# One transfer for the first pair's query weights in a cached-attention decode kernel

## The chip, the core and the metric

The kernel runs on one core of one Trainium2 chip. The metric is the device time of one launch in microseconds (us); lower is better. All data are 32-bit floats.

## What is computed

One decode step of a block: layer norm of x, grouped-query attention over a long key and value cache, and beside it a dense layer with the Mish activation; both are added to x.

```python
B, D = 8, 512                       # 8 sequences, one token each
Hq, Hkv, Sk, Dh = 32, 8, 8192, 128  # 4 query heads share one key head
F = 1792

xn = layernorm(x)
q = xn @ wq                                   # wq: 512 x 4096
scores = q . k_cache / sqrt(Dh)               # k_cache: 8 x 8 x 8192 x 128
o = softmax(scores) . v_cache                 # v_cache: the same shape
a = o @ wo                                    # wo: 4096 x 512
h = xn @ w1 + b1
m = (h * tanh(softplus(h))) @ w2
out = x + a + m
```

## The kernel before

**Units and buffers.** The caches hold 512 MB in all, and every byte is read once. The work is cut into 32 units (`UNITS`): unit j takes a pair of key heads (m = j // 8) and one sequence (b = j % 8). A unit's keys are one transfer of 8 MB (128 partitions of 64 KB, `load_unit(kT, ...)`, L131), and its values another. All these transfers are issued by the sync engine (SP), which takes its instructions in order and stops at one whose semaphores are not yet there. One large tile `kv` has room for two and a half such transfers: values at `V_AT`, keys in turn at `K_AT[0]` and `K_AT[1]`, which overlap by half. So the keys of unit j + 1 are issued when half the scores of unit j are done (`scores` is called in two halves), and the values of unit j when the values of unit j - 1 are used up.

**The start is different.** The keys of unit 0 go to the values' place. The first weights of the dense layer, `w1` (3.5 MB, L476), go to the start of `K_AT[0]`'s place, where x and its centred copy `xc` stand until then; its bias `b1` comes through four small GpSimd transfers (L147). The keys of unit 1 go to `K_AT[1]` and the values of unit 0 (in the loop over units) to `V_AT`, when the scores of unit 0 have read the keys there. On SP the order is: first pair's query weights, keys 0, `w1`, keys 1, values 0, keys 2, values 1 and so on.

**The queries.** For each pair of heads, `project(m)` multiplies xn by a 512 x 1024 slice of `wq`, `spread` lays the result out in `qr`, and `key_weights` makes from it the stationary operand `wk` of unit j's scores. For the pairs 1 to 3 the slice comes by `load_q(m)` (L125): one SP transfer of 2 MB into `ws`, 128 partitions of 16 KB, so that partition p holds rows 4p to 4p + 3 of the slice; `project` takes four terms with the transposed activations `xn4`. For pair 0 the slice is split. Rows 0 to 383 come by an SP transfer of 1.5 MB into `ws` (L153, three rows to a partition). Rows 384 to 511 come by four GpSimd transfers of 128 KB (L150), issued in turn with the four for `b1`, into `q0_x`: partitions 64 to 95 of `kv` (`XQ`), four rows to a partition, at the column `XAT`. This is the start of `K_AT[1]`'s place, so the transfer of keys 1 waits until `project(0)` has read `q0_x`. The seven terms of pair 0 take the activations from two further transposed copies, `xn3` and `xnx`, which TensorE and VectorE make beside `xn4` (L208 to L221).

**The rest of a unit.** `softmax`, `values` (for the unit before), `key_weights` (for the next unit), `turn` (transposes the exponentials into the stationary operand `pt8` of the values) and `merge`. In unit 0 the activation of the dense layer, `mish` (L399 to L446), stands between; it uses the place of `w1` as scratch, and keys 2 go there afterwards. After the last unit come the transfers of `wo` and `w2` and two output products.

**Where the work starts.** GpSimd builds an identity and `perm` by memsets behind its eight transfers (L158 to L161); VectorE derives masks from them, and then computes the norm (L188 to L201) together with ScalarE.

Of the kernel before, what the change touches and what calls it, by code (L numbers as in the profile page):

```python
# [8 lines left out]
F32 = mybir.dt.float32  # L9
# [4 lines left out]
P = 128  # L14
B = 8
# [12 lines left out]
BW = 1024  # L28
CC = D // P
# [8 lines left out]
ROW = NB * P * BW // P  # L38
# [10 lines left out]
NJ = PL * HALF  # L49

W2R = 7

D3 = 3
XQ = slice(64, 96)
XAT = ROW + ROW // 2

# [11 lines left out]
def kernel(  # L72
# [12 lines left out]
    nc = tc.nc  # L85
    PSUM = bass.MemoryType.PSUM

    const = ctx.enter_context(tc.tile_pool(name="const", bufs=1))
# [4 lines left out]
    kv = const.tile([P, PLACES], F32, name="kv")  # L93
    ws = const.tile([P, CC * BW], F32, name="ws")
# [4 lines left out]
    M = psum.tile([P, 512], F32, name="m")  # L99
    H = psum.tile([P, 512], F32, name="h")  # L100

    ident = const.tile([P, P], F32, name="ident")
# [7 lines left out]
    gsel = const.tile([B, B, B], F32, name="gsel")  # L110
    xn4 = const.tile([P, CC, B], F32, name="xn4")
    xnT = const.tile([P, CC, B], F32, name="xnT")
    xn3 = const.tile([P, D3, B], F32, name="xn3")
    xnx = const.tile([P, CC, B], F32, name="xnx")
    qr = const.tile([P, DI, H2 * B], F32, name="qr")
    xres = const.tile([P, P], F32, name="xres")
    oT = const.tile([P, NP, H2, B], F32, name="oT")
# [4 lines left out]
    def load_q(m):  # L122

        rows = wq.rearrange("j p f -> (j p f)").rearrange("(m p f) -> m p f", m=NP, p=P)
        nc.sync.dma_start(ws, rows[m])  # L125

    def load_unit(src, j, at):
        m, b = divmod(j, B)
        lo = (b * HKV + 2 * m) * NH * G
        t = kv[:, at : at + ROW]  # L130
        nc.sync.dma_start(  # L131
            t,
            src[lo : lo + NB].rearrange("j p f -> (j p f)").rearrange("(p f) -> p f", p=P),
        )
        return t
# [3 lines left out]
    x_sb, xc, sq = (low[:, i * D : (i + 1) * D] for i in range(3))  # L139
    nc.scalar.dma_start(x_sb, x)  # L140
    b1_sb = kv[:B, W1_AT + 7168 : W1_AT + 7168 + FG // 2]
    q0 = wq[:CC].rearrange("j p f -> (j p) f")
    q0_3 = ws[:, : D3 * BW]
    q0_x = kv[XQ, XAT : XAT + CC * BW]
    for r in range(4):
        n = FG // 8
        nc.gpsimd.dma_start(  # L147
            b1_sb[:, n * r : n * (r + 1)], b1.rearrange("(g c f) -> c g f", g=B, c=4)[r]
        )
        nc.gpsimd.dma_start(  # L150
            q0_x[r::4], q0[D3 * P :].rearrange("(e r i) f -> r e (i f)", r=4, i=CC)[r]
        )
    nc.sync.dma_start(q0_3, q0[: D3 * P].rearrange("(p i) f -> p (i f)", i=D3))  # L153
    k_t = {0: load_unit(kT, 0, V_AT)}
    w1_t = kv[:, W1_AT : W1_AT + 7168].rearrange("p (j f) -> p j f", j=2 * CC)

# [47 lines left out]
    for c in range(CC):  # L204
        nc.tensor.transpose(
            M[:, 32 + c * B : 32 + (c + 1) * B], xc[:, c * P : (c + 1) * P], ident[:B, :B]
        )
    for c in range(D3):  # L208
        nc.tensor.transpose(
            M[:, 64 + c * B : 64 + (c + 1) * B], xc[:, c : D3 * P : D3], ident[:B, :B]  # L210
        )
    for c in range(CC):
        nc.tensor.matmul(
            M[XQ, 96 + c * B : 96 + (c + 1) * B],
            xc[:, D3 * P + c :: CC],
            ident[:B, :B],
            start=True,
            stop=True,
        )
    nc.vector.tensor_copy(xn3.rearrange("p c b -> p (c b)"), M[:, 64 : 64 + D3 * B])  # L220
    nc.vector.tensor_copy(xnx[XQ].rearrange("p c b -> p (c b)"), M[XQ, 96:128])  # L221
    nc.vector.tensor_copy(xn4.rearrange("p c b -> p (c b)"), M[:, 0:32])
    nc.vector.tensor_copy(xnT.rearrange("p c b -> p (c b)"), M[:, 32:64])
    for g in range(G):
# [4 lines left out]
            start=True,  # L229
            stop=True,  # L230
# [14 lines left out]
    def project(m):  # L245

        w = ws.rearrange("p (c f) -> p c f", c=CC)
        terms = [(c, xn4[:, c, :], w[:, c]) for c in range(CC)]
        if m == 0:
            wx = q0_x.rearrange("p (c f) -> p c f", c=CC)  # L250
            terms = [(c, xn3[:, c, :], w[:, c]) for c in range(D3)]
            terms += [((c + D3) % CC, xnx[XQ, c, :], wx[:, c]) for c in range(CC)]
        for d in range(2):
            for n, (c, xt, wt) in enumerate(terms):
                nc.tensor.matmul(  # L255
                    H[Q * c : Q * c + B, :],
                    xt,
                    wt[:, d * 512 : (d + 1) * 512],
                    start=(n < CC),
                    stop=(n >= len(terms) - CC),  # L260
                )
            qp = work.tile([P, 512], F32, name="e")
            nc.scalar.copy(qp, H)
            for h in range(REP):
                at = 192 + (d * REP + h) * B
                nc.tensor.matmul(  # L266
                    M[:, at : at + B],
                    qp[:, h * DH : (h + 1) * DH],
                    bsel[:, :B],
                    start=True,  # L270
                    stop=True,
                )
        qT = work.tile([P, H2 * B], F32, name="qT", bufs=1)
        nc.vector.tensor_scalar_mul(qT, M[:, 192 : 192 + H2 * B], DH**-0.5)
        return qT
# [199 lines left out]

    nc.sync.dma_start(w1_t, w1.rearrange("j p f -> p j f"))  # L476
    qT = project(0)
    k_t[1] = load_unit(kT, 1, K_AT[1])
    spread(qT)
# [3 lines left out]
    for j in range(UNITS):  # L483
        b = j % B
# [23 lines left out]
        if more and b == MAKE_Q:  # L508
            qT = project(j // B + 1)
# [29 lines left out]
    for g in range(G):  # L539
# [4 lines left out]
            start=False,  # L544
            stop=False,
# [44 lines left out]
```

## Time and profile before

| | |
|---|---|
| median of three runs | 1333.28 us (1331.31 to 1333.68) |
| the profiled execution | span of 1330.5 us from first to last instruction; the runs shown are 0.8 to 3.2 us above it, their median 2.8 us |
| moved from and to memory | 561.79 MB, a mean of 422 GB/s over the span |
| TensorE busy with matmuls | 984.8 us, 74% |
| VectorE busy | 516.0 us, 39% |
| ScalarE, GpSimd busy | 40.2 us, 6.4 us |

In the profile PE is TensorE (PEld its weight loads), DVE VectorE, ACT ScalarE, POOL GpSimd, SP the sync engine; SPq stands for an instruction that SP issues, and L131 is line 131 of the kernel. A row of the timeline has its start and its length in us, then engine, line, operation, what is written and read, and how many instructions were merged in the row; in brackets follows how long the engine had been idle and what released it. A row of the windows has the stretch, its length, the busy time of each engine (with the number of instructions), the granted TensorE clock, the busy share of the 16 DMA engines, and what they moved in GB/s; bytes are put down where a packet ends, so short stretches scatter. A row of transfers has the count, the size of each and the median time from issue to landing.

### The profile page before, as it was taken

To read this page: it belongs to the slowest core of one execution; us is meant where nothing else is said; L and a number is where in the kernel's file an instruction comes from. 1 tells how busy PE (TensorE), PEld (TensorE's weight loads), DVE (VectorE), ACT (ScalarE), POOL (GpSimd) and SP (SyncE) were. 2 spreads that over 40 slices of the span, in tenths; PEclk is the share of its full clock that TensorE was granted. 3 is DMA by queue.
4 is the path that set the end of the run, shared out by engine and by line. 5 is a ranking of instruction groups with operands and counts; after the bars stand their busy time and mean duration, and the time that the engine had idled before them with its cause. 6 is when DMAs were issued, how large, how long until landed. Compare 5 with 4: busy or idle time off the path is not lost.

```text
span 1330.5 us, 11234 instructions
## 1 busy us (share of the span) xinstructions
PE 984.8 (74%) x5071; PEld 338.3 (25%) x5071; DVE 516.0 (39%) x730; ACT 40.2 (3%) x88; POOL 6.4 (0%) x17
## 2 busy tenths in 40 slices
PE   1888776877867976776887777687786787677766
PEld 0422222222322222222322222222232222222222
DVE  2065444134443234444244444413444332444431
ACT  1000000000000000000000000000000000000000
POOL 1000000000000000000000000000000000000000
PEclk9999789988889888879988888998897998888898
DMA  9889999999999999999999999999999999999997
GB/s 341 338 346 432 420 438 436 436 428 436 428 436 434 434 432 428 427 439 438 426 432 432 438 430 434 426 438 434 430 430 434 432 434 436 428 428 434 430 415 321
DMA packets 13839, 561.79 MB, mean 422 GB/s; under 512 B 1464, under 2 KB 1592, under 8 KB 4800
## 3 DMA queue, kind: packets, MB, share of 16 engines
q1 hardware_dynamic: 13520, 560.53, 98.2%
q8 instruction: 39, 0.64, 0.2%
q0 software_dynamic: 256, 0.53, 0.1%
q10 hardware_dynamic: 16, 0.02, 0.0%
q14 instruction: 8, 0.07, 0.0%
HBM read 561.01 MB, written 0.07 MB: 422 GB/s over the span
## 4 chain that ended last, share of the span: by engine, by line
DMA 73%; PE 22%; DVE 2%; SPq 2%; issue 0%; POOL 0%; ACT 0%; DVEq 0%; POOLq 0%
DMA kv<-in_v 70%; PE o L378 19%; DMA kv<-in_wq 2%; DMA kv<-in_w 2%; SPq L528 2%; PE s L316 1%; DVE pt L366 1%; PE x L281 1%; PE h L255 0%; PE m L266 0%; PE h L403 0%; DVE kv L434 0%; DVE tr L360 0%; POOL kv L147 0%; DVE wk L299 0%
## 5 line engine op out<-in xcount | busy, mean ns | idle before, releaser
L316 PE MATMUL s<-kv,wk 128*64 128x512 f32 x2048 | 505.7, 657 | 180.7 <-DMA kv<-in_kT 178.1
L378 PE MATMUL o<-kv,pt 128*32 128x512 f32 x2048 | 262.3, 671 | 51.8 <-DMA kv<-in_v 42.2
L316 PEld LDWEIGHTS s<-kv,wk 128*64 128x64 f32 x2048 | 156.0, 152 | 505.0 <-issue 321.5
L366 DVE TENSOR_REDUCE pt<-tr 64x512 f32<-64x2048 f32 x64 | 241.3, 3771 | 1.6
L328 DVE TENSOR_REDUCE nm<-s 128x1 f32<-128x512 f32 x32 | 22.1, 692 | 374.2 <-PE s L316 374.1
L355 PE MATMUL x<-e,perm 128*128 128x512 f32 x256 | 126.4, 639 | 2.0 <-ACT qr L288 2.0
L378 PEld LDWEIGHTS o<-kv,pt 128*32 128x32 f32 x2048 | 68.4, 122 | 219.3 <-issue 164.9
L386 DVE TENSOR_SCALAR os<-o,isel 128x128 f32<-128x128 f32 x32 | 11.2, 351 | 265.4 <-PE o L378 265.4
L360 DVE STREAM_TRANSPOSE tr<-x 128x512 f32<-128x512 f32 x128 | 78.6, 671 | 0.0
L299 DVE TENSOR_TENSOR wk<-qr,mask 128x512 f32<-128x512 f32 x64 | 63.0, 1026 | 19.8 <-ACT qr L288 19.8
L355 PEld LDWEIGHTS x<-e,perm 128*128 128x128 f32 x256 | 48.9, 201 | 74.6 <-issue 72.2
L347 ACT ACTIVATE e<-s,nmx 128x512 f32<-128x512 f32 x32 | 22.0, 688 | 1092.8 <-DVE nmx L344 1092.8
L388 DVE SCALAR_TENSOR_TENSOR os<-o,isel,os 128x128 f32<-128x128 f32 x96 | 33.7, 351 | 3.4
L329 PE MATMUL m<-ident,nm 128*1 128x128 f32 x32 | 8.7, 273 | 30.1 <-DVE nm L328 30.1
L340 PE MATMUL m<-ident,nx 1*128 1x1 f32 x32 | 7.0, 219 | 24.2 <-DVE nx L336 24.2
L281 PE MATMUL x<-qT,tr 128*128 128x64 f32 x128 | 19.3, 315 | 3.0 <-ACT qr L288 2.7
L358 DVE RECIPROCAL rt<-m 128x8 f32<-128x8 f32 x32 | 6.6, 208 | 34.0 <-PE m L356 34.0
L281 PEld LDWEIGHTS x<-qT,tr 128*128 128x128 f32 x128 | 18.1, 226 | 6.2 <-ACT qr L288 3.3
L395 PE MATMUL m<-hsel,os 128*128 128x8 f32 x64 | 12.4, 266 | 9.3 <-DVE rt L358 9.3
L349 DVE TENSOR_SCALAR lsel<-rsel,l 128x8 f32<-128x8 f32 x32 | 7.4, 231 | 30.1 <-ACT e L347 30.1
L329 PEld LDWEIGHTS m<-ident,nm 128*1 128x1 f32 x32 | 2.5, 79 | 58.3 <-DVE nm L328 58.3
L356 PEld LDWEIGHTS m<-lsel,ones 128*128 128x128 f32 x64 | 12.2, 190 | 15.6 <-issue 15.3
(98 smaller groups left out, 172.2 us busy)
## 6 DMA issues: line engine op xcount, KB each, us to landing
kv<-in_wo SPq DMA_DIRECT2D x4, 2048.0 KB, 25.9
ws<-in_wq SPq DMA_DIRECT2D x3, 2048.0 KB, 35.2
kv<-in_w SPq DMA_DIRECT2D x1, 3584.0 KB, 24.7
kv<-in_w SPq DMA_DIRECT2D x1, 2048.0 KB, 37.0
ws<-in_wq SPq DMA_DIRECT2D x1, 1536.0 KB, 7.6
kv<-in_w SPq DMA_DIRECT2D x1, 1024.0 KB, 20.7
kv<-in_kT SPq DMA_DIRECT2D x32, 29.5
kv<-in_wq POOLq DMA_DIRECT2D x4, 128.0 KB, 25.1
```

Of the source, the lines that this page charges most:

```text
L281: nc.tensor.matmul(X[:, half, k * 64 : (k + 1) * 64], wide[:, half * 8 + k], qT, start=True, stop=True,)
L299: nc.vector.tensor_mul(w[:, :, d], q[:, :, d].to_broadcast([P, DI, NH * G, REP]), mask[:, d * NH * G : (d + 1) * NH * G] .rearrange("p (o ...
L316: nc.tensor.matmul(S[64 * c : 64 * (c + 1), :], w[:, i].rearrange("p d k h -> p (d k h)"), kk[:, i, c, :], start=(part == 0 and n == 0), s ...
L328: nc.vector.tensor_reduce(nm, S, axis=AX.X, op=ALU.max, negate=True)
L347: nc.scalar.activation(e, S, AF.Exp, bias=nmx, accum_out=l)
L355: nc.tensor.matmul(X[:, g], perm[:, g], e, start=True, stop=True)
L360: nc.vector.transpose(tr.rearrange("p (l t) c -> p t l c", t=TL)[:, tl], X.rearrange("p g (t q l) -> p t l g q", t=TL, q=PP)[:, tl],)
L366: nc.vector.tensor_reduce(pt8[half, :, :, d * REP : (d + 1) * REP].rearrange("p c y h -> p y c h"), tr[half].rearrange("p y (g c h) -> p y ...
L378: nc.tensor.matmul(O[Q * q : Q * (q + 1), :], pt8[:, c, TL * l : TL * (l + 1), :].rearrange("p t h -> p (t h)"), vt[:, 512 * n : 512 * (n ...
L388: nc.vector.scalar_tensor_tensor(os, O[:, DH * i : DH * (i + 1)], isel[:, i : i + 1], os, op0=ALU.mult, op1=ALU.add)
L395: nc.tensor.matmul(M[:, 168 : 168 + H2], os, hsel, start=True, stop=True)
L528: nc.sync.dma_start(t, w2_rows[:, lo * BW : hi * BW])
```

## The change

`load_q(0)` takes the place of the transfer of 1.5 MB and of the four of 128 KB; `q0_x`, `xn3`, `xnx`, the three transposes and four small products that fill them, their two copies, and the seven terms of pair 0 go. `project(0)` then has the four terms of the other pairs. The four small transfers of `b1` stay with GpSimd. The order of everything else is unchanged.

```diff
-D3 = 3
-XQ = slice(64, 96)
-XAT = ROW + ROW // 2
...
-    xn3 = const.tile([P, D3, B], F32, name="xn3")
-    xnx = const.tile([P, CC, B], F32, name="xnx")
...
-    q0 = wq[:CC].rearrange("j p f -> (j p) f")
-    q0_3 = ws[:, : D3 * BW]
-    q0_x = kv[XQ, XAT : XAT + CC * BW]
+    load_q(0)
     for r in range(4):
         n = FG // 8
         nc.gpsimd.dma_start(
             b1_sb[:, n * r : n * (r + 1)], b1.rearrange("(g c f) -> c g f", g=B, c=4)[r]
         )
-        nc.gpsimd.dma_start(
-            q0_x[r::4], q0[D3 * P :].rearrange("(e r i) f -> r e (i f)", r=4, i=CC)[r]
-        )
-    nc.sync.dma_start(q0_3, q0[: D3 * P].rearrange("(p i) f -> p (i f)", i=D3))
     k_t = {0: load_unit(kT, 0, V_AT)}
...
-    for c in range(D3):
-        nc.tensor.transpose(
-            M[:, 64 + c * B : 64 + (c + 1) * B], xc[:, c : D3 * P : D3], ident[:B, :B]
-        )
-    for c in range(CC):
-        nc.tensor.matmul(
-            M[XQ, 96 + c * B : 96 + (c + 1) * B],
-            xc[:, D3 * P + c :: CC],
-            ident[:B, :B],
-            start=True,
-            stop=True,
-        )
-    nc.vector.tensor_copy(xn3.rearrange("p c b -> p (c b)"), M[:, 64 : 64 + D3 * B])
-    nc.vector.tensor_copy(xnx[XQ].rearrange("p c b -> p (c b)"), M[XQ, 96:128])
...
-        if m == 0:
-            wx = q0_x.rearrange("p (c f) -> p c f", c=CC)
-            terms = [(c, xn3[:, c, :], w[:, c]) for c in range(D3)]
-            terms += [((c + D3) % CC, xnx[XQ, c, :], wx[:, c]) for c in range(CC)]
```

## Prediction

> **What bounds the kernel now.** I read first the slices of the page and its chain of waits, then windows of the stretches in which the slices are low, then the first 112 us instruction by instruction.
>
> ```profile
> GB/s 341 338 346 432 420 438 436 436 428 436 428 436 434 434 432 428 427 439 438 426 432 432 438 430 434 426 438 434 430 430 434 432 434 436 428 428 434 430 415 321
> ```
> ```profile
> DMA 73%; PE 22%; DVE 2%; SPq 2%; issue 0%; POOL 0%; ACT 0%; DVEq 0%; POOLq 0%
> ```
>
> ```profile
> 27.00:34.00 7.00, 0.00 (x0) 0.00 (x0) 0.00 (x0) 0.00 (x0) 0.00 (x0) 1.00 0.78 220
> 34.00:39.00 5.00, 4.25 (x19) 2.04 (x22) 0.00 (x0) 0.59 (x1) 0.00 (x0) 1.00 1.03 406
> 39.00:42.50 3.50, 3.14 (x14) 0.12 (x8) 0.00 (x0) 0.29 (x1) 0.00 (x0) 1.00 0.40 161
> 43.00:61.50 18.50, 14.86 (x54) 10.33 (x56) 2.17 (x3) 1.17 (x2) 0.00 (x0) 1.00 1.08 451
> 61.50:73.00 11.50, 11.06 (x52) 3.37 (x48) 0.39 (x1) 0.00 (x0) 0.00 (x0) 1.00 0.02 6
> ...
> 112.00:1250.00 1138.00, 863.43 (x4314) 292.17 (x4313) 451.03 (x619) 29.61 (x70) 0.00 (x0) 0.88 1.00 432
> ```
>
> From 112 us on the DMA engines are always busy (share 1.00) and move 432 GB/s; the chain is 73% DMA. There the time is bytes over rate, and no engine matters. Only the first 73 us are below that, as the page's first three slices show: a slow stretch from 27 to 34 (220 GB/s), a hole at 39 to 42.5, and nothing at all from 61.5 to 73. The bytes that must come before values 0 (query weights, keys 0, `w1`, keys 1: 2.10 + 8.39 + 3.67 + 8.39 = 22.55 MB) would take 52.2 us at 432 GB/s and took until 73. What is saved there moves everything behind it forward, since the rest runs at the DMA's own rate.
>
> The holes come from SP's order:
>
> ```profile
> 0.74 0.38 SPq L153 DMA_DIRECT2D ws<-in_wq  x1
> 1.19 0.42 SPq L131 DMA_DIRECT2D kv<-in_kT  x1
> 17.63 0.38 SPq L476 DMA_DIRECT2D kv<-in_w  x1
> 42.20 0.34 SPq L131 DMA_DIRECT2D kv<-in_kT  x1
> 72.60 0.33 SPq L131 DMA_DIRECT2D kv<-in_v  x1
> 90.79 0.33 SPq L131 DMA_DIRECT2D kv<-in_kT  x1
> 111.55 0.33 SPq L131 DMA_DIRECT2D kv<-in_v  x1
> ```
>
> ```profile
> SPq L131 <- PE s L316: 30.0, 1, 30.0
> SPq L131 <- DMA kv<-in_wq: 15.9, 2, 14.6
> ```
>
> Keys 1 (issue at 42.20) stood behind the four small transfers and then behind the products that read them (L255), since they share a place; values 0 (72.60) stood 30.0 us behind the scores of unit 0. Both waits have one origin:
>
> ```profile
> ws<-in_wq SPq DMA_DIRECT2D x1, 1536.0 KB, 7.6
> ```
> ```profile
> kv<-in_wq POOLq DMA_DIRECT2D x4, 128.0 KB, 25.1
> ...
> kv<-in_b POOLq DMA_DIRECT2D x4, 1.8 KB, 21.2
> ```
>
> The 1.5 MB from SP landed 7.6 us after issue, at 8.3; the 128 KB transfers of GpSimd had a median of 25.1 us, and even 1.8 KB of `b1` took 21.2, while the 8 MB of keys 0 flowed. The last was there at about 34, and TensorE began then:
>
> ```profile
> 17.45 1.89 PE L255 MATMUL h<-ws,xn 128*8 128x512 f32 x6
> 34.05 1.89 PE L255 MATMUL h<-kv,xnx 32*8 32x512 f32 x8 [14.71 <-DMA kv<-in_wq]
> ...
> 38.43 1.89 PE L255 MATMUL h<-ws,xn 128*8 128x512 f32 x6
> 40.25 1.89 PE L255 MATMUL h<-kv,xnx 32*8 32x512 f32 x8
> ...
> 55.72 16.84 PE L316 MATMUL s<-kv,wk 128*64 128x512 f32 x64 [2.65 <-DVE wk L299]
> ```
>
> **The change, part by part.**
> *The transfer of the weights.* 2 MB instead of 1.5 first in SP's queue: 7.6 x 4/3 = 10.1 us at most in proportion, so it lands at about 11, before its reader. The trace has no 2 MB transfer into an empty queue; the near bound is 7.6 us, the far one the later pairs' 35.2 us (row below), which are issued behind megabytes in flight. I take 10.1, nearest to the row of the same place and queue; the far end is the last rival.
>
> ```profile
> ws<-in_wq SPq DMA_DIRECT2D x3, 2048.0 KB, 35.2
> ```
>
> *GpSimd's queue.* Its rows, and VectorE's that waits for it:
>
> ```profile
> 1.91 0.52 POOL L150 DMA_DIRECT2D kv<-in_wq  x1
> ```
> ```profile
> 6.72 0.99 DVE L169 COPY perm<-ident 128x16 f32<-128x16 f32 x8 [4.23 <-POOL perm L160]
> ```
>
> Four issues of 0.52 us go from ahead of the memsets; VectorE's setup had waited 4.23 us for `perm`, so the setup and the norm start 4 x 0.52 = 2.1 us earlier.
>
> *Transposes and copies.*
>
> ```profile
> 15.09 0.46 PE L209 MATMUL m<-ident,kv 8*128 8x8 f32 x3
> ```
> ```profile
> 16.16 0.18 DVE L220 COPY xn<-m 128x24 f32<-128x24 f32 x1 [2.12 <-PE m L213]
> ```
>
> The transposes that go start at 15.09, and the copies waited for the last product of L213 until 16.16: about 0.9 us behind the transposes that stay, which end near 15.25. The two copies that go add 0.2 each ahead of the others. I take 1.25 us in all. With the 2.1 the first product of `project(0)` moves from 17.45 to 14.1, and `w1`, which waits for the last reader of x at the same place, from 17.63 to 14.3.
>
> *`project(0)`.* It no longer waits for a transfer: start at 14.1 instead of 34.05. From there to the scores it took 55.72 - 34.05 = 21.67 us; the second half now has one group of products instead of two, which saves 40.25 - 38.43 = 1.82. So the scores of unit 0 start at 14.1 + 19.85 = 33.95. Cover: keys 0 must be there, at about 27 plus some 3 of landing (next paragraph).
>
> *Keys 1.* With `q0_x` gone nothing holds them; SP issues them right behind `w1`, at about 14.7. No hole at 39 to 42.5.
>
> *Values 0.* The scores took 72.60 - 55.72 = 16.88 us up to the issue: 33.95 + 16.88 = 50.8. From keys 1, whose 8.39 MB lie in the window 43.0 to 61.5 (451 GB/s) after an issue at 42.20, data start some 0.9 us after an issue into an empty queue: 51.7, if the queue is empty.
>
> *Is it empty?*
>
> ```profile
> 1.50:16.50 15.00, 1.94 (x19) 1.85 (x19) 6.18 (x29) 3.35 (x5) 6.00 (x13) 1.00 1.06 398
> ```
>
> The bytes ahead: 398 GB/s for 15 us from 1.5 on (5.97 MB), the other 4.52 MB of the query weights and keys 0 at 432 (10.5 us, to 27.0), `w1` at the 406 GB/s of the window 34 to 39, in which only it flowed (9.0 us, to 36.0), keys 1 at 432 (19.4 us, to 55.4). So the queue is not empty at 51.7: values 0 follow at 55.4 without a gap. Before, they started at 72.60 + 0.9 = 73.5. The gain is 73.5 - 55.4 = 18.1 us, and now it is the DMA that ends last, with 3.7 us to spare for TensorE. That margin is also the cover of the two early edits: without their 2.1 and 1.25 us values 0 would still flow at 55.1, and nothing is lost.
>
> *Does it last?* What comes next hangs on values 0's issue through the engines, or on landings: keys 2 issue 18.2 us behind values 0's issue (90.79 - 72.60, held by `mish`), so at 69.0, well before values 0 have flowed (55.4 + 19.4 = 74.8); values 1 issue at most 39.0 behind (111.55 - 72.60), 89.8, before keys 2 end at 94.2. Scores of unit 1 need keys 1, landing near 59, at 60.6 at the earliest. So no hole opens, and the shift stands to the end.
>
> Sum: span 1330.5 - 18.1 = 1312.4; with the 2.8 us by which the median lies above the span, **1315.2 us**. A change of 0.2% (2.7 us) is about what a measurement here can tell from none.
>
> *Bounds.* Best: all 22.55 MB at the best rate shown (451) from 1.5 on end at 51.5, and values 0 flow at 51.7: a gain of 21.8, 1311.5. Worse: if the rates of 27 to 34 and the tail at 39 to 42.5 belong to `w1` (eight pieces of 3.5 KB to a partition), and not to the small transfers, 7.0 x (1 - 220/432) + 2.2 = 5.6 us are lost again: 1320.8. The end of the kernel speaks against it: there `wo` follows the values in pieces of 4 KB, at a rate near the 406.
>
> ```profile
> 1290.00:1310.00 20.00, 10.43 (x78) 2.65 (x82) 10.72 (x10) 0.00 (x0) 0.00 (x0) 0.74 0.97 393
> ```
>
> *A rule of the skill against it.* The Trainium skill, "DMA: Bandwidth & Descriptors", Specifications, gives about 358 GB/s of memory bandwidth to a core. By it the 22.55 MB would end at 1.5 + 63.0 = 64.5 and the gain be 9.0 us (1324.3). The trace's 432 over 1138 us says that this core, alone on its memory, is not so limited.
>
> **The rivals.**
> *Start-up stays slow* (the worse bound above): 1320.8. For it: `w1` began to flow in that stretch. Against: `w1` alone ran at 406, and the end rows.
>
> *Scores of unit 0 become the bound.* At the start TensorE is slow: eight records of L255 take 1.89 us at 34 and 1.04 in the next pair; the 64 of unit 0's scores took 16.84, of unit 1's 13.95, so they were slow in part.
>
> ```profile
> 260.15 1.04 PE L255 MATMUL h<-ws,xn 128*8 128x512 f32 x8
> ```
> ```profile
> 82.30:96.30 14.00, 13.95 (x64) 4.50 (x64) 1.00 0.98 417
> ```
>
> Slow throughout they take 13.95 x 1.89/1.04 = 25.4 us; values 0 would flow at 33.95 + 25.4 + 0.9 = 60.3: a gain of 13.2, 1320.1. Against: 16.84 in the trace, after the same work as will precede it. The Trainium skill, "TensorE: Matmul & The Clock Gate", Part 1, says the slow state ends after a window of some 3.4 us of sustained activity, at no fixed phase; by that it would not last, which lowers this chance.
>
> *The gain is given back.* If something not tied to values 0 held keys 2 or values 1 near 90.79 and 111.55, a hole would open and the time stay 1333.3. Against: keys 2 waited for `mish`, which follows the scores of unit 0.
>
> *Slower: the weights land late.* The whole of `ws` is now one transfer on SP, with 8 MB right behind it on the same engines; if parts of it only finish with what follows, as the later pairs' do in 35.2 us, `project(0)` waits for all. Values 0 issue 19.85 + 16.88 = 36.7 us behind that landing: from a landing at 35.9 on it is slower than before. Landing with `w1`, which came 24.7 us after its issue at 17.63, at 42.3, values 0 would issue at 79.0, 6.4 us late: 1339.7. Against: the 1.5 MB in the same place landed in 7.6 us although keys 0 were issued 0.45 us behind.
>
> ```profile
> kv<-in_w SPq DMA_DIRECT2D x1, 3584.0 KB, 24.7
> ```
>
> **How the numbers follow.** As summed 0.80 (its own range 1312.0 to 1318.0); start-up slow 0.09; scores the bound 0.04; the skill's memory limit 0.01; given back 0.03; late weights 0.03. The first four are faster: 0.94; same 0.03; slower 0.03. The range goes from 1312.0 to 1321.0, which takes in the first three.
>
> **What would show it.** Right: project(0) without a wait near 14; keys 1 issued near 15; values 0 near 51; no window below 380 GB/s between 5 and 110 us; and the first three slices near 400 or more. Wrong: a landing of `ws` beyond 14; a stretch near 220 GB/s with `w1` in flight and no GpSimd transfer of weights; scores of unit 0 longer than 20 us; or a hole behind keys 2 or values 1.

## The result and the profile after

The changed kernel takes 1313.16 us in the median of four runs (1312.59 to 1313.51), the kernel before 1332.3 beside it. The ratio is 0.9854, 95% interval 0.984 to 0.9868: 19.1 us faster. Measured once more on another chip it took 1313.12 against 1331.26, ratio 0.9862 (0.9848 to 0.9877). The profiled execution took 1312.88 us with a span of 1311.1; the span of before was 1330.5. In the code after the change the line numbers are lower: `project`'s products are L223 (before L255), the scores L284 (L316), the values' products L346 (L378), `load_unit` L123 (L131), `w1`'s transfer L444 (L476).

The page's slices: the first three are no longer below the rest by a fifth.

```profile
GB/s 393 450 420 440 428 436 428 431 440 428 437 428 436 428 439 424 443 424 438 426 435 438 423 440 422 442 426 434 436 431 434 432 432 432 430 431 432 425 415 326
```

SP's queue in the first 130 us:

```profile
0.74 0.38 SPq L117 DMA_DIRECT2D ws<-in_wq  x1
1.19 0.42 SPq L123 DMA_DIRECT2D kv<-in_kT  x1
14.28 0.38 SPq L444 DMA_DIRECT2D kv<-in_w  x1
14.71 5.46 SPq L123 DMA_DIRECT2D kv<-in_kT  x1
50.67 0.33 SPq L123 DMA_DIRECT2D kv<-in_v  x1
68.85 0.33 SPq L123 DMA_DIRECT2D kv<-in_kT  x1
89.54 0.33 SPq L123 DMA_DIRECT2D kv<-in_v  x1
```

Keys 1 are issued at 14.71 instead of 42.20, values 0 at 50.67 instead of 72.60. TensorE:

```profile
14.10 1.90 PE L223 MATMUL h<-ws,xn 128*8 128x512 f32 x8
...
33.97 16.66 PE L284 MATMUL s<-kv,wk 128*64 128x512 f32 x64 [2.64 <-DVE wk L267]
```

`project(0)` starts at 14.10 without a wait. The transfers of the first microseconds (issue to landing, last column), and the first window:

```profile
ws<-in_wq SPq DMA_DIRECT2D x1, 2048.0 KB, 8.0
kv<-in_b POOLq DMA_DIRECT2D x4, 1.8 KB, 7.6
```
```profile
1.50:16.50 15.00, 3.48 (x24) 1.22 (x24) 8.25 (x31) 3.79 (x6) 3.94 (x9) 1.00 1.04 421
```

The weights land at 8.7. Even `b1` now needs 7.6 us and not 21.2, though it stays with GpSimd and beside keys 0. And values 0 land 26.0 us after their issue, since bytes of keys 1 are still ahead of them:

```profile
kv<-in_v SPq DMA_DIRECT2D x1, 26.0
```

That is at 76.7. Before it was at 95.7 (issue 72.60, and 23.1 us into an empty queue): 19.0 us earlier, which is nearly all of the 19.4 us by which the span fell.

### The profile page after: what moved, and what is told of

It reads as the page before. It is cut to its first block, busy times and chain, and to the rows that moved or that the text cites. A ratio compares the mean times of both kernels' runs of the same rounds, so it can differ in the third digit from the quotient of the medians.

```text
span 1311.1 us, 11174 instructions
## 1 busy us (share of the span) xinstructions
PE 995.4 (76%) x5048; PEld 341.6 (26%) x5048; DVE 515.6 (39%) x728; ACT 40.2 (3%) x88; POOL 4.4 (0%) x13
## 4 chain that ended last, share of the span: by engine, by line
DMA 72%; PE 23%; DVE 2%; SPq 2%; issue 0%; ACT 0%; POOL 0%; POOLq 0%; DVEq 0%
DMA kv<-in_v 70%; PE o L346 20%; DMA kv<-in_w 2%; SPq L496 2%; PE s L284 1%; DVE pt L334 1%; PE x L249 1%; PE m L234 0%; PE h L223 0%; PE h L371 0%; DVE kv L402 0%; DVE tr L328 0%; DVE wk L267 0%; POOL kv L137 0%; DVE nm L296 0%
## 5 line engine op out<-in xcount | busy, mean ns | idle before, releaser
L284 PE MATMUL s<-kv,wk 128*64 128x512 f32 x2048 | 509.7, 661 | 171.2 <-DMA kv<-in_kT 168.6
L346 PE MATMUL o<-kv,pt 128*32 128x512 f32 x2048 | 267.9, 683 | 49.1 <-DMA kv<-in_v 39.6
L284 PEld LDWEIGHTS s<-kv,wk 128*64 128x64 f32 x2048 | 157.0, 153 | 498.5 <-issue 324.5
L323 PE MATMUL x<-e,perm 128*128 128x512 f32 x256 | 130.8, 658 | 2.0 <-ACT qr L256 2.0
L346 PEld LDWEIGHTS o<-kv,pt 128*32 128x32 f32 x2048 | 69.3, 123 | 221.3 <-issue 169.5
L323 PEld LDWEIGHTS x<-e,perm 128*128 128x128 f32 x256 | 50.8, 209 | 76.9 <-issue 74.5
## 6 DMA issues: line engine op xcount, KB each, us to landing
kv<-in_w SPq DMA_DIRECT2D x1, 1024.0 KB, 20.7
kv<-in_w SPq DMA_DIRECT2D x1, 512.0 KB, 20.7
```

Source lines behind the costliest of these rows:

```text
L284: nc.tensor.matmul(S[64 * c : 64 * (c + 1), :], w[:, i].rearrange("p d k h -> p (d k h)"), kk[:, i, c, :], start=(part == 0 and n == 0), s ...
L323: nc.tensor.matmul(X[:, g], perm[:, g], e, start=True, stop=True)
L346: nc.tensor.matmul(O[Q * q : Q * (q + 1), :], pt8[:, c, TL * l : TL * (l + 1), :].rearrange("p t h -> p (t h)"), vt[:, 512 * n : 512 * (n ...
```

## Experiments

Two theories share the gain: the wait (late weights, hence late scores, hence late values 0) and the DMA itself (the start moves its bytes faster). Against both stands a third: that keys 1, held by the shared place, were the loss. The comparisons give the median beside runs of the kernel before on the same chip.

**GpSimd again, but into `ws`.** Late weights without a hold on keys 1.

```diff
-    load_q(0)
+    q0 = ...                                    # first pair's slice, 128 rows of 16 KB
+    nc.sync.dma_start(ws[:64], q0[:64])
+    nc.sync.dma_start(ws[96:], q0[96:])
     for r in range(4):
         ...                                     # b1, as before
+        nc.gpsimd.dma_start(ws[64:96][r::4], q0[64:96][r::4])
```

> The changed kernel, but a quarter of the first pair's weights (partitions 64 to 95 of ws, 512 KB) comes again by four GpSimd transfers of 128 KB, as before; they go to ws and not to the place of keys 1, so keys 1 are not held. Theory (the late landing of the GpSimd transfers delays project(0), hence the scores of unit 0, hence values 0): they land near 34 again, keys 1 issue near 20 or earlier, the scores start at 34.05 + 19.85 = 53.9, values 0 issue at 70.8, and the DMA stands idle from about 56 to 71. The time is 20.1 - 2.4 = 17.7 us above the changed kernel, near 1331, hardly better than before. Rival (it was the hold on keys 1 that cost, the hole at 39 to 42.5 and what follows): with that gone most of the gain stays, at or below 1320.

Measured 1333.93 us (before 1332.34), ratio 1.0008 (0.9999 to 1.0017): all of the gain is gone.

```profile
16.75 10.88 SPq L123 DMA_DIRECT2D kv<-in_kT  x1
71.03 0.33 SPq L123 DMA_DIRECT2D kv<-in_v  x1
```
```profile
35.84 1.90 PE L226 MATMUL h<-ws,xn 128*8 128x512 f32 x8 [19.62 <-DMA ws<-in_wq]
```
```profile
62.00:73.00 11.00, 9.45 (x48) 2.93 (x48) 1.32 (x5) 0.00 (x0) 0.00 (x0) 1.00 0.25 89
```

Keys 1 go out at 16.75, but TensorE waits 19.62 us for the weights, values 0 go out at 71.03, and the DMA stands idle before that. The hold on keys 1 was a hole that cost nothing; the rival falls.

**Both parts by SP, everything else as before.** The old shape, its places and its seven terms, without GpSimd.

```diff
     nc.sync.dma_start(q0_3, ...)
+    nc.sync.dma_start(q0_x, q0[D3 * P :].rearrange("(p i) f -> p (i f)", i=CC))
...
-        nc.gpsimd.dma_start(q0_x[r::4], ...)
```

> The kernel before with its two parts, its seven terms and its extra transposes, but the 512 KB to the place of keys 1 come by one SP transfer right behind the 1.5 MB instead of four from GpSimd. Theory (the queue matters, not the shape): both parts land near 9, project(0) starts at 17.45 - 2.1 = 15.4 and takes one group of products more in each half, scores start at 15.4 + 1.8 + 21.7 = 38.9, values 0 issue at 55.7 and flow at 56.6, where the changed kernel's flow near 54.0: 2.6 us slower than the changed kernel, near 1315.8. Rival (the split shape, with its 32 partitions and the place shared with keys 1, is what costs): near 1325 or more.

Measured 1315.68, ratio 0.9874 (0.9859 to 0.9889). The number came out, its reason did not:

```profile
kv<-in_kT SPq DMA_DIRECT2D x1, 33.9
```
```profile
1.50:16.50 15.00, 3.57 (x33) 2.09 (x33) 7.47 (x33) 3.37 (x5) 3.96 (x9) 1.00 1.00 351
...
42.50:55.00 12.50, 12.05 (x58) 3.66 (x54) 0.40 (x1) 0.00 (x0) 0.00 (x0) 1.00 0.99 430
55.00:62.00 7.00, 5.90 (x54) 2.13 (x55) 4.07 (x11) 2.06 (x3) 0.00 (x0) 1.00 1.00 431
```

There is no hole in front of values 0 (issued at 54.59). Keys 1, issued at 25.40, landed at 59.3, where the changed kernel has them at 57.3 (14.71 + 42.6): the first 15 us moved 351 GB/s and not 421. Keys 0 already landed at 30.3, 2.3 us later than in the changed kernel (28.0), so the loss lies in the first 30 us. The queue makes most of the gain, but the shape has a price too; two runs below take it up.

**Keys 0 in smaller packets.** GpSimd as before; the 64 KB rows of keys 0 become four transfers of 16 KB rows.

```diff
-    k_t = {0: load_unit(kT, 0, V_AT)}
+    for i in range(4):                          # n = ROW // 4
+        nc.sync.dma_start(kv[:, V_AT + n * i : V_AT + n * (i + 1)], k0[:, n * i : n * (i + 1)])
+    k_t = {0: kv[:, V_AT : V_AT + ROW]}
```

> The kernel before, GpSimd transfers and all, but keys 0 come by four SP transfers of a quarter of the columns each, so that their packets are 16 KB and not 64 KB. Theory (each packet of a GpSimd transfer waits for its turn behind one packet of SP's queue on the same engine, 2.4 us for 64 KB): a turn is a quarter as long, the GpSimd weights land within 7 to 10 us of issue, by about 15; project(0) starts at 17.45 without a wait, scores at 17.45 + 1.8 + 21.7 = 41, values 0 issue at 57.8 and flow at 58.7: 4.7 us above the changed kernel, near 1318. Rival (GpSimd transfers are slow by themselves, whatever stands beside them): they land near 34 again and the time stays near 1332.

Measured 1321.57, ratio 0.9917 (0.9902 to 0.9932).

```profile
kv<-in_wq POOLq DMA_DIRECT2D x4, 128.0 KB, 11.6
kv<-in_b POOLq DMA_DIRECT2D x4, 1.8 KB, 9.9
```
```profile
20.76 1.89 PE L259 MATMUL h<-kv,xnx 32*8 32x512 f32 x8 [1.43 <-DMA kv<-in_wq]
```

The GpSimd weights take 11.6 us instead of 25.1, the last are there at 20.7 instead of 34, yet later than the 15 of the theory, and the time is 3.6 us above its 1318. So what flows beside them decides, by its packets; but four times smaller ones made it only 2.2 times faster, so turns of one packet are not the whole of it. The Trainium skill, "DMA: Bandwidth & Descriptors", Queues, rings and completion order, says that each engine goes round its queues packet by packet; this run agrees in direction.

**Keys 0 held back** until the GpSimd weights have landed.

```diff
+    nc.sync.dma_start(out[64:96], q0_x[:, :P])  # waits for q0_x; written over at the end
     k_t = {0: load_unit(kT, 0, V_AT)}
```

> The kernel before, GpSimd transfers and all, but SP first sends 16 KB of the weights of partitions 64 to 95 on to the output array (overwritten at the end), so that keys 0 are issued only when the GpSimd weights have landed. Theory (it is the packets of keys 0 beside them that delay the GpSimd weights): they land by about 9 and not 34; keys 0 flow from about 12; project(0) starts at 17.45 without a wait; scores at about 41 (keys 0 land near 35), values 0 issue at 57.8; the other bytes (20.5 MB) end at 12 + 47.5 = 59.5: values 0 flow at 59.5, some 5.5 us above the changed kernel, near 1318.7, although the DMA stands nearly idle for several us at the start. Rival (GpSimd transfers are slow by themselves): they land at 25 or later, keys 0 follow only then, and the time is 1345 or more.

Measured 1317.65, ratio 0.9893 (0.9876 to 0.9909).

```profile
kv<-in_wq POOLq DMA_DIRECT2D x4, 128.0 KB, 5.9
```
```profile
10.22 0.36 SPq L154 DMA_DIRECT2D out<-kv  x1
10.63 0.41 SPq L131 DMA_DIRECT2D kv<-in_kT  x1
```

Without keys 0 beside them the same four transfers take 5.9 us and are there by 10.2. Keys 0 start 9.4 us later than before, and the kernel is 13.9 us faster. GpSimd's transfers are not slow by themselves.

**ScalarE's queue** instead of GpSimd's for the four transfers (`nc.scalar.dma_start`).

> The kernel before, but the four transfers of 128 KB are issued by ScalarE's queue instead of GpSimd's; same places, same sizes. Theory (any second queue takes turns with SP's 64 KB packets): the rows are 16 KB packets now, fewer turns; with one data packet and one closing packet for each of four transfers on an engine, 4 to 8 turns of 2.4 us, a landing at 12 to 22; values 0 issue at 56 to 61, and the time is 3 to 8 us above the changed kernel, 1316 to 1321. Rival (only GpSimd's transfers are slow): landing under 10, 1315.8 as with one SP transfer. Rival (a second queue starves until SP's queue is empty): landing beyond 30, near 1331.

Inconclusive. Ten runs lie between 1321.67 and 1334.46, median 1328.44, ratio 0.997 (0.9948 to 0.9993). All are above the range of the turns (1316 to 1321), and five, from 1330.88 up, lie where the last rival put them. In the profiled one, at 1323.21, `project(0)` waited for the weights until 23.8, 2 us beyond the range of the turns. A second queue beside keys 0 is late also when it is not GpSimd's, and by how much varies from run to run; why was not found.

**Scores later by known amounts.** The changed kernel with extra memsets on VectorE ahead of its setup, 8 and then 22.

```diff
-    for t in (H, O, M):
+    for t in (H, O, M) + (H,) * 8:              # and 22
         nc.vector.memset(t, 0.0)
```

> The changed kernel with eight more memsets of 0.54 us on VectorE at the start; less the 2.2 us that VectorE waits there anyway, all compute up to the scores of unit 0 comes 2.1 us later, values 0 issue at 52.8. Theory (the DMA queue before values 0 ends near 54 and sets the time; compute has a margin of about 2.4 us): no change, 1313.2 within 0.5. Rival (the scores set the start of values 0): 2.1 us slower, 1315.3.

> The same with 22 more memsets: 22 x 0.54 - 2.2 = 9.7 us later, values 0 issue at 60.4 and flow at 61.3, where the queue is empty from 54.0 on. Theory: the margin is used up and the rest counts one for one: 7.3 us slower than the changed kernel, 1320.5. Rival (a late start is made up later, because the DMA has slack in the steady part): no more than 2 us slower. Rival (no margin): 9.7 us, 1322.9.

Measured 1314.29 and 1322.83 (before 1331.51), ratios 0.9868 (0.9854 to 0.9883) and 0.9931 (0.9916 to 0.9946). With 8 memsets values 0 go out at 52.88, no hole opens there, and they land at 76.9, 0.2 us later than in the changed kernel. Yet the median is 1.1 us up, beyond the 0.5 of the theory, as is the span (1312.2); the intervals overlap, so it is small beside the noise. A first place to look is one unit later, where TensorE computes unit 0's values (first row the changed kernel, second row with 8 memsets), and then the window behind, in the same order:

```profile
81.03 8.44 PE L346 MATMUL o<-kv,pt 128*32 128x512 f32 x64
```
```profile
83.21 9.95 PE L346 MATMUL o<-kv,pt 128*32 128x512 f32 x64
```
```profile
92.00:94.00 2.00, 1.61 (x7) 0.87 (x5) 1.69 (x4) 0.00 (x0) 0.00 (x0) 1.00 0.81 336
```
```profile
92.00:94.00 2.00, 2.00 (x14) 0.61 (x7) 0.70 (x2) 0.00 (x0) 0.00 (x0) 1.00 0.38 164
```

The products started 2.2 us later and took 1.5 longer; values 1 went out at 93.23 instead of 89.54, and the window dropped to 164 GB/s. But so short a window scatters (the repeat of the changed kernel, the last run below, has 262 there), and the landings show that little was lost. Issue to landing of values 1, again in the same order:

```profile
kv<-in_v SPq DMA_DIRECT2D x1, 26.4
```
```profile
kv<-in_v SPq DMA_DIRECT2D x1, 22.3
```

That is 115.9 and 115.5. The scores of unit 3, which wait for keys 3, start 0.4 us later (135.70 against 135.30); most of the rest arises at the very end, in the products with `w2`:

```profile
1303.77 1.93 PE L435 MATMUL h<-kv,aT 128*8 128x128 f32 x64 [1.22 <-DMA kv<-in_w]
```
```profile
1304.16 3.58 PE L435 MATMUL h<-kv,aT 128*8 128x128 f32 x64 [2.89 <-DMA kv<-in_w]
```

With 22 memsets TensorE started 11.9 us later (more than the 9.7 that I had reckoned), values 0 went out at 61.97, and a hole stands there:

```profile
56.00:62.00 6.00, 5.92 (x28) 1.68 (x24) 0.03 (x1) 0.00 (x0) 0.00 (x0) 1.00 0.00 0
```

An issue 11.3 us later made values 0 land 8.6 us later (85.3): the margin there is 2.7 us. The median rose by 9.7, so the rest of the kernel makes up nothing. That this gives the 1322.9 of the rival without a margin is chance, since its delay was 9.7 and not 11.3.

**Narrow pieces on SP.** The changed kernel, its 2 MB cut by partitions, then, as a control, cut by columns.

```diff
-    load_q(0)
+    nc.sync.dma_start(ws[:64], q0[:64])         # by partitions
+    nc.sync.dma_start(ws[96:], q0[96:])
+    nc.sync.dma_start(ws[64:96], q0[64:96])
```

```diff
-    load_q(0)
+    for lo, hi in ((0, 2 * BW), (2 * BW, 3 * BW), (3 * BW, 4 * BW)):
+        nc.sync.dma_start(ws[:, lo:hi], q0[:, lo:hi])   # by columns
```

> The changed kernel with the same 2 MB to the same places, but by three SP transfers: partitions 0 to 63, 96 to 127, 64 to 95. It differs from the run with GpSimd transfers into ws only in the queue of the last. Theory A (transfers to few partitions flow slower, and that is the 2.5 us by which the kernel with two SP parts was above the changed one, its keys 1 having landed 2 us later): the first 16.5 us move 325 to 360 GB/s instead of 421, keys 1 land near 59, 1315.5. Rival B (those 2.5 us came from the scores, which were 3.9 us later there): here the scores start when they do in the changed kernel, 1313.2.

> The changed kernel with the 2 MB of weights by three SP transfers of 1 MB, 512 KB and 512 KB, as in the run with the narrow piece on SP, but each over all 128 partitions (a half and two quarters of the columns). Theory (few partitions make a transfer slow): the first 16.5 us move 400 GB/s or more, and the time is that of the changed kernel, 1313.2 within 1. Rival (it was the number of transfers): 280 to 330 GB/s in the first 16.5 us, and 1317.8 again.

Measured 1317.8, ratio 0.9894 (0.9879 to 0.9909), and 1313.32, ratio 0.9866 (0.985 to 0.9883). The window from 4 to 10 us, by partitions and by columns:

```profile
4.00:10.00 6.00, 0.00 (x0) 0.00 (x0) 3.72 (x19) 1.63 (x3) 1.53 (x4) 1.00 1.03 213
```
```profile
4.00:10.00 6.00, 0.00 (x0) 0.00 (x0) 3.72 (x19) 1.64 (x3) 1.52 (x4) 1.00 1.04 414
```

The engines are as busy (share 1.03 and 1.04) and move half. Values 0 went out at 50.01, no later than in the changed kernel, and landed at 81.4, 4.7 us later, so all of the 4.6 us is DMA. That is more than either theory of the first run gave. Not the number of transfers but their few partitions cost it. The Trainium skill, "SBUF — State Buffer", Door 1, says that bandwidth hangs on how many of 16 ports the partitions reach, and by its table 0 to 63 reach eight and 64 to 127 the other eight; 213 beside 414 agrees.

**Long rows.** What is left of the start and the end is bytes over rate, and `w1` and `wo` come in short pieces. Their layout in memory is changed, not the amount.

```diff
-    nc.sync.dma_start(w1_t, w1.rearrange("j p f -> p j f"))
+    nc.sync.dma_start(kv[:, W1_AT : W1_AT + 7168], w1)   # 28 KB to a partition
...
-        nc.sync.dma_start(w_o[m].rearrange(...), wo[4 * m : 4 * (m + 1)].rearrange(...))
+        nc.sync.dma_start(w_o[m], wo[m])                 # 16 KB to a partition
```

> The changed kernel with w1 and wo laid out in memory so that a partition's part is one row (28 KB and 16 KB) instead of pieces of 3.5 and 4 KB. Theory (the DMA's bytes over rate set the time from the first byte on, and w1 and wo flow at 409 and 406 to 415 GB/s where long rows flow at 432): 3.67 MB save 0.5 us and 8.39 MB 1.2 us, 1.7 us in all, 1311.5 where the changed kernel has 1313.2. Rival (the end is set by the chain of products behind the last transfers, and the start by values 1): under 0.5 us.

> The changed kernel again, beside the two others on the same chip: 1313.2, within 1.

Measured 1311.67, ratio 0.9851 (0.9837 to 0.9866), beside 1313.12, ratio 0.9862 (0.9848 to 0.9877), for the changed kernel; the four runs of the one (1311.28 to 1312.06) lie below those of the other (1312.67 to 1313.7), though the intervals of the ratios overlap. While `w1` flows, the changed kernel and then this one:

```profile
27.00:34.00 7.00, 3.71 (x18) 3.53 (x18) 1.93 (x2) 1.17 (x2) 0.00 (x0) 1.00 1.01 408
```
```profile
27.00:34.00 7.00, 3.73 (x18) 3.54 (x18) 1.93 (x2) 1.17 (x2) 0.00 (x0) 1.00 1.03 442
```

By the medians that is 1.5 us of the expected 1.7; by the profiled executions only 0.7 (spans of 1310.2 and 1310.9). There values 1 land 0.5 us earlier (115.1 against 115.6) and the first part of `w2`, behind `wo`, 1.2 us earlier (1302.4 against 1303.6); slower last products give 0.5 back. The direction is shown, the exact size is not. It is the fastest version here.

## Why the prediction was right, and where it was off

- **The steps in time** came out: `project(0)` at 14.10 (14.1), `w1` issued at 14.28 (14.3), scores at 33.97 (33.95), values 0 issued at 50.67 (50.8), keys 2 at 68.85 (69.0), values 1 at 89.54 (89.8). The weights landed at 8.7, earlier than taken.
- **That the DMA then ends last** was right: values 0 took 26.0 us from issue to landing, 2.9 more than into an empty queue. With late compute the time rose, so the shift did stand to the end.
- **The rival of the slow start** fell: in the window from 27 to 34 the DMA moves 408 GB/s where it moved 220, and `w1` lands at 37.0 instead of 42.3. The low rate belonged to the weights' transfers, not to `w1`.
- **The other rivals** fell as well: the weights were not late (8.7), the scores of unit 0 took 16.66 us and not 25.4, and keys 2 and values 1 went out as reckoned. Why TensorE is slow at the start no run shows: in the prediction's row from 43.0 to 61.5 the granted clock is 1.00. Of the signs, "no window below 380" holds for long windows only; 39.0 to 42.5 has 318, behind 567 from 34 to 39.
- **The size**: 1315.2 against 1313.16. Of the 2.0 us, 1.3 lie in the span (1312.4 against 1311.1). The term that was mis-sized is the first 15 us, taken at the 398 GB/s of the profile before; they moved 421, 0.35 MB more or 0.8 us. The 398 held traffic of GpSimd and to few partitions, which the change removes, so the row was the wrong one for it. Of the 0.5 us left in the span, 0.4 arose behind values 0 (they landed 19.0 us earlier, and the span fell by 19.4); no run shows where. The other 0.7 us is the step from the span to the median: I took 2.8 us from before, it is 2.1 after. In every run on record the time is 1.7 to 1.9 us above the span of the same run, so the 2.8 held a full microsecond of scatter between the profiled execution and the median of three.
- **A margin that was too large, without harm**: the 3.7 us "to spare for TensorE" measure 2.7 at values 0. So the sentence that without the two early edits (3.35 us) "nothing is lost" does not hold: some 0.6 us would be, an estimate from the 2.7.
- **What I costed at nothing by not seeing it**: that a transfer over few partitions slows the DMA. I put the gain on waits alone. With the wait gone, the old shape on SP still cost 2.5 us and three narrow pieces 4.6. The first figure is explained only in part: 512 KB at 213 instead of 414 GB/s cost 1.2 us more, an estimate from these two rows.

## What to carry to other kernels

Where a kernel is bound by its bulk transfers, look for the moment at which they first stand idle, and follow the wait back to the smallest transfer in it: 512 KB on a second queue, beside an 8 MB stream with 64 KB rows, held up the whole kernel by 16.7 us (1332.34, against 1315.68 with the same two parts on SP). Put what is needed first into the bulk queue itself, ahead of the stream and over all partitions. When a wait is gone, measure the margin by adding known delays, and read what a delay costs from the landings of the bulk transfers: a window of 2 us can show a hole that they do not.

## What was not expected of the hardware

- SP's own issue can block. Keys 1's issue took 5.46 us behind `w1`'s pieces of 3.5 KB (0.33 to 0.42 at SP's other issues above). With `w1` and `wo` in long rows it took 0.43, and the three issues of `w2` at the end 1.42 us together instead of 21.33:

```profile
14.65 0.43 SPq L123 DMA_DIRECT2D kv<-in_kT  x1
...
1266.06 1.42 SPq L493 DMA_DIRECT2D kv<-in_w  x3
```

  The short pieces alone do not set it: behind the same `w1`, keys 1's issue took 0.94 us in the run by columns, 0.57 with 22 memsets and 10.88 with GpSimd into `ws`. What does was not found. Behind keys 1 nothing was waiting on SP. At the end the last products of the changed kernel wait 0.32 and 0.17 us for the second and third part of `w2`, so there it may have cost up to 0.5 us.
- Transfers to 64 or 32 partitions moved 213 GB/s at a full busy share, where all 128 moved 414.
